# Block sums of V on TensorE, a first layer split 2, 3, 3, 4, and a floor under weights in an attention and two-layer MLP kernel

## The chip, the cores and the metric

The kernel runs on one core of one Trainium2 chip. The metric is device time in microseconds of one execution. Five engines work side by side, each on its own queue in order: TensorE (PE, with its weight loads as PEld), VectorE (DVE), ScalarE (ACT), GpSimd (POOL) and SyncE (SP), which here only starts transfers.

## The reference

The first stage is attention over 768 positions, for 2 batches of 8 heads of 64: each query sees the keys nearer than 16 positions, and 24 summaries, one per block of 32 positions (the maximum of the block's keys, the mean of its values). Two MLP layers follow on the 1536 tokens of width 512. The weights come as 64-bit floats.

```python
k_sum = k.reshape(B, H, nb, block, D).max(axis=3)
v_sum = v.reshape(B, H, nb, block, D).mean(axis=3)
...
scores_s = scores_s + np.log(block)
scores_l_m = np.where(mask_l, scores_l, -1000000000.0)
scores_all = np.concatenate([scores_l_m, scores_s], axis=-1)
...
a = a / (np.sum(a, axis=-1, keepdims=True) + 1e-09)
return np.matmul(a, v_all).astype(np.float32)
...
g = x @ w_gate
silu = g * (1.0 / (1.0 + np.exp(-g)))
val = x @ w_val
return (silu * val @ w_out).astype(np.float32)
...
h = x @ w_in
relu6 = np.clip(h + 3.0, 0.0, 6.0)
g = h * relu6 / 6.0
return (g @ w_out).astype(np.float32)
```

## The kernel before

**Attention.** Four tiles of 384 queries (two per batch), and in each four pairs of heads. A pair goes through: `scores` (24 matmuls on TensorE, tile `at_s`; `kT`, `ksum` and the queries, `acc` or `qT`), `top` (VectorE adds the mask and takes each row's extremum, six times), `exp` (ScalarE, six times), `norm` (VectorE), `weigh` (GpSimd multiplies P), `turn` (TensorE transposes P, `at_t`), `pt_put` (ScalarE copies it to `pt`), `outputs` (12 matmuls of P^T with the values `vw`, tile `pv`: a PV), and the output's split into `x` (ScalarE copies the high part, VectorE takes the rest). Per batch and pair there are also the maximum of the keys (`ksum`, VectorE) and the summaries of the values: VectorE sums V (`total`, tile `v`), TensorE turns the sums (`mm_v`, `at_v`), and ScalarE or VectorE copies them into `vw`.

**MLP.** Every product is made of three matmuls of high and low parts (`three`, L368 to L370), so that fp32 accuracy is kept. Layer one has 12 blocks of 128 hidden units, done in 4 groups of 3 blocks; the first group runs on the four tiles of 384 tokens as attention gives them, the other three on three tiles of 512. Layer two has 16 blocks in 4 groups of 4.

**Weights** (`weights`). A block of 128x512 64-bit values is loaded (`raw`, 3 buffers) and turned to fp32 bits (`bits`, 2 buffers) by steps on VectorE: the exponent (L405), the sign (L411), the tail (L415) and a guard (L423) that multiplies by 0 where the magnitude, which ScalarE takes in place (L419), is below 2^-15. Then the high part is copied and the low part taken (`wa` or `wb`, one ring per group in turn; `wb` exists only from the `swap` on, when attention's buffers are given up).

**The order.** Nothing runs in the order in which it is written. Every step is a task with a rank and a guess of its duration per engine; a planner (`Plan`) takes, engine by engine, the task that can start first, and of those the one of lowest rank, six rounds over. The instructions are issued in the order that comes out. Ranks come from the constants at the head (`LEAD`, `SPAN`, ...). Where the plan has TensorE idle in the first 60 us it puts dummy matmuls on zeros (L812).

Of the kernel before, what the change touches and what calls it, by code (L numbers as in the profile page):

```python
# [15 lines left out]
P = 128  # L16
# [17 lines left out]
F1, G1 = 1536 // P, 3  # L34
F2, G2 = 2048 // P, 4
N1, N2 = F1 // G1, F2 // G2
NEG = 1.0e9
SCALE = 1.0 / D**0.5


LEAD = dict(
    w_load=5.21, k_load=6.88, v_load=8.44, q_load=7.36, vw_load=1.00, keys=3.87, values=0.53, queries=2.61,
    k_put=1.0, v_put=1.0, q_put=1.0, top=3.0, exp=3.0, norm=4.0, weigh=4.0, turn=4.0, pt_put=4.0,
)
LAG = 2.58
MASKS = -5.01
PAIR_GAP = 4.06
MAIN = 28.05
W_FIRST = 6.44, 0.80
W_REST = 18.53, 3.46  # L50
SPAN = 12.44
NEXT, NEXT_END = -3.40, 23.95
NEXT_W = 7.71
W_END = 15.26
LATE = 0.90
# [3 lines left out]
BIAS = dict(dve=.4)  # L59
# [3 lines left out]
def consts():  # L63

    import numpy as np

    a = np.zeros((P, P + 3 * NK), np.float32)  # L70
# [29 lines left out]
class Task:  # L100
    __slots__ = ("engines", "port", "rank", "fn", "deps", "takes", "uses", "end", "engine", "start")


class Plan:
# [15 lines left out]
    def add(self, rank, engines, fn, r=(), w=(), after=(), port=False):  # L120
# [5 lines left out]
        t.port = {"pool": True, "dve": port}  # L126
        t.engines, t.rank, t.fn, t.end, t.takes = engines, rank, fn, None, []
# [46 lines left out]
    def schedule(self, rank):  # L174
# [14 lines left out]
        free, order, held = {}, [], {}  # L189
        while pool:  # L190
# [20 lines left out]
            s, t, e = best  # L211
            t.start, t.engine, t.end = s, e, s + t.engines[e]
# [68 lines left out]
def tile_kernel(ctx: ExitStack, tc: tile.TileContext, q, k, v, vu, w_gate, w_val, w_out1, w_in2, w_out2, cst, out):  # L281
    nc = tc.nc
    rings = dict(mm=4, mmb=4, at=3, pv=1, wa=9, wb=9, raw=3, bits=2, u=3, g=4, gb=5,
                 v3=1, qT=4, p=4, st=2, pt=4)
# [27 lines left out]
    for n in ("v3", "qT", "p", "st", "pt"):  # L312
        pools[n] = ab_p

    tiles = {}
    pv_bank = pools["pv"].tile([P, T], F32, name="pv")
# [17 lines left out]
    cs = cpool.tile([P, P + 3 * NK], F32, name="cs")  # L334
# [11 lines left out]
    def tiles_of(layer, g):  # L346
        nb = TB if (layer, g) == (0, 0) else WIDE
        return [(b0, nb) for b0 in range(0, BLOCKS, nb)]
# [9 lines left out]
    def three(rank, bk, n, lhs, rhs, n_k, reads, early=False):  # L358
# [35 lines left out]
    def weights(rank, layer, g, i, f, after):  # L394
# [4 lines left out]
        def load():  # L399
            src = w_src(layer, i, g * (G1, G2)[layer] + f)  # L400
# [57 lines left out]
    def hidden1(rank, g, t, f, late):  # L458
# [14 lines left out]
        for i, bk in enumerate((bg, bv)):  # L473
# [6 lines left out]
                early=g == 0 and b0 == 0,  # L480
# [7 lines left out]
    def out1(rank, g, t, d, late):  # L488
# [6 lines left out]
            G1,  # L495
# [4 lines left out]
        room = [("A", b0 // TB)] + [("q0", t, c) for t in range(2) for c in range(NP) if q_room(t, c) == b0 // TB] if g == 0 else []  # L500
# [49 lines left out]
    def out2(rank, g, t, m, late, d0=0, n=DM):  # L550
        if (g, m, n) == (N2 - 1, BLOCKS - 1, DM):
# [9 lines left out]
            G2,  # L561
# [22 lines left out]
    vw = [ap_.tile([NK, NB, P], F32, name=f"vw{c}") for c in range(NP)]  # L584
# [16 lines left out]
    def v_room(b, c):  # L601
        return c if b == 0 else 2 + c % 2

    def load_v(b, c):
        vn[b, c] = acc_room(v_room(b, c), 0, S)
        nc.sync.dma_start(out=vn[b, c], in_=v[b, c])

    def load_vw(t, c):
        b, half = divmod(t, 2)
        u0, to = half * NB, vw[c]  # L610
        nc.sync.dma_start(out=to[NS + HALO : NS + HALO + QB], in_=vu[b, c, :, u0 + 1 : u0 + 1 + NB])
        nc.sync.dma_start(out=to[NS : NS + HALO], in_=vu[b, c, QB - HALO :, u0 : u0 + NB])
        nc.sync.dma_start(out=to[NS + HALO + QB :], in_=vu[b, c, :HALO, u0 + 2 : u0 + 2 + NB])

    def keys(rank, b, c):
# [14 lines left out]
    def values(rank, b, c):  # L630
# [10 lines left out]

        def put(e):
            copy(e, vw[c][:NS], tiles[ps].unsqueeze(1).to_broadcast([NS, NB, P]), 1.0 / BLOCK)

        add(rank, {"dve": 0.87}, total, r=[room], w=[v3])
        add(rank, {"pe": 0.12}, turn, r=[v3, ("cs",)], w=[ps, ("vs", c)])
        add(rank - LEAD["v_put"], {"act": 0.69, "dve": 0.86}, put, r=[ps], w=[("vs", c)])

    def queries(rank, t, c):
        n = ("qT" if t > 1 else "q0", t, c)  # L650
        b, half = divmod(t, 2)

        def load():
            if t < 2:
                tiles[n] = acc_room(q_room(t, c), S + c % 2 * T, T)
            else:
                new(n, [P, T])
            second(t, c).dma_start(out=tiles[n], in_=q[b, c, :, half * T : (half + 1) * T])

        add(rank - LEAD["q_load"], {"dma": 0.68}, load, w=[n])  # L660

    def scores(rank, t, c):

        b, half, qt = t // 2, t % 2, ("qT" if t > 1 else "q0", t, c)
# [21 lines left out]
        for j in range(TR):  # L686
            add(rank, {"pe": 0.37}, lambda j=j: go(j), r=[("kT", b, c), ("ksum", c), qt],
# [230 lines left out]
```

## Time and profile before

| | |
|---|---|
| median of 3 runs | 632.81 us (632.78 to 635.15) |
| the profiled execution | 632.16 us, span of its instructions 630.4 us |
| TensorE busy | 618.9 us (98% of the span) |
| VectorE busy | 426.7 us (68%) |
| ScalarE busy | 269.2 us (43%) |
| GpSimd busy | 51.5 us (8%) |
| read from HBM, written | 50.19 MB, 3.15 MB |

Busy times are means over stages that differ; a duration of a matmul includes the part that lies under its neighbours, so what one costs is read from the distance of two starts. Dummy matmuls count as busy.

### The profile page before, as it was taken

What the parts mean: (1) busy time and instruction counts of PE and PEld (TensorE: products, weight loads), DVE (VectorE), ACT (ScalarE), POOL (GpSimd) and SP (SyncE); (2) the same over time, 40 slices, a digit from 0 to 9 for tenths busy, and PEclk for the clock granted to TensorE, in tenths of its full rate; (3) what the DMA queues carried; (4) which work ended last, traced back from release to release, by engine and by line L of the source; (5) the groups of instructions that cost most, each with busy time, mean ns of one, the idle gap of its engine ahead of it and who ended that gap; (6) DMA issues with size and microseconds to landing.
All of it is one profiled execution on the core that took longest, in us unless ns stands there. A gap on an engine that the chain in (4) does not pass through costs nothing.

```text
span 630.4 us, 10224 instructions
## 1 busy us (share of the span) xinstructions
PE 618.9 (98%) x3976; PEld 523.1 (83%) x3976; DVE 426.7 (68%) x881; ACT 269.2 (43%) x594; POOL 51.5 (8%) x55
## 2 busy tenths in 40 slices
PE   8899999999999999999999999999999999999997
PEld 7787889998888888888888888888888888888886
DVE  5999954799999847595739978565758553344332
ACT  4896886465545323242225444544523331132120
POOL 1333423001010000000000110000000000000000
PEclk9999999999999999999999999999999999999999
DMA  9887241233432403022011412030301000000103
GB/s 321 262 277 234 71 129 44 68 133 135 137 130 101 165 2 100 1 100 101 33 35 34 134 34 73 31 131 11 123 1 67 1 2 0 1 0 1 67 18 116
DMA packets 18912, 53.99 MB, mean 86 GB/s; under 512 B 2608, under 2 KB 5168, under 8 KB 18864
## 3 DMA queue, kind: packets, MB, share of 16 engines
q1 hardware_dynamic: 18576, 52.74, 24.7%
q8 instruction: 31, 0.51, 0.3%
q10 hardware_dynamic: 288, 0.61, 0.3%
q14 instruction: 17, 0.14, 0.1%
HBM read 50.19 MB, written 3.15 MB: 85 GB/s over the span
## 4 chain that ended last, share of the span: by engine, by line
PE 91%; DVE 5%; DMA 3%; issue 0%; ACT 0%
PE mm L368 16%; PE mm L369 15%; PE mm L370 15%; PE mmb L368 13%; PE mmb L369 13%; PE mmb L370 13%; PE at_s L681 2%; DMA kT<-in_k 1%; DMA raw<-in_moe_w_val 1%; PE pv L752 1%; PE at_t L738 1%; DVE p L701 1%; DVE bits L415 1%; DVE wa L302 0%; DVE ksum L623 0%
## 5 line engine op out<-in xcount | busy, mean ns | idle before, releaser
L368 PE MATMUL mm<-x,wa 128*128 128x384 f32 (+1 forms) x168 | 63.5, 378 | 0.0
L369 PE MATMUL mm<-x,wa 128*128 128x384 f32 (+1 forms) x168 | 61.0, 363 | 1.4 <-DVE wa L302 1.4
L370 PE MATMUL mm<-x,wa 128*128 128x384 f32 (+1 forms) x168 | 60.9, 362 | 0.0
L419 ACT ACTIVATE raw<-raw 128x512 f32<-128x512 f32 x68 | 46.0, 678 | 33.2 <-DVE bits L411 33.0
L415 DVE SCALAR_TENSOR_TENSOR bits<-raw,bits 128x512 uint32<-128x512 uint32 x68 | 48.8, 722 | 0.1
L423 DVE SCALAR_TENSOR_TENSOR bits<-raw,bits 128x512 f32<-128x512 f32 x68 | 47.6, 704 | 0.8
L411 DVE SCALAR_TENSOR_TENSOR bits<-raw,bits 128x512 uint32<-128x512 uint32 x68 | 46.5, 685 | 0.7
L369 PE MATMUL mmb<-x,wb 128*128 128x512 f32 x120 | 46.7, 389 | 0.0
L370 PE MATMUL mmb<-x,wb 128*128 128x512 f32 x120 | 46.7, 389 | 0.0
L368 PE MATMUL mmb<-x,wb 128*128 128x512 f32 x120 | 46.7, 389 | 0.0
L368 PE MATMUL mm<-x,wb 128*128 128x512 f32 x120 | 46.7, 389 | 0.0
L369 PE MATMUL mm<-x,wb 128*128 128x512 f32 x120 | 46.7, 389 | 0.0
L370 PE MATMUL mm<-x,wb 128*128 128x512 f32 x120 | 46.7, 389 | 0.0
L708 ACT ACTIVATE p<-p,st 128x120 f32<-128x120 f32 x96 | 36.6, 383 | 5.1 <-DVE st L701 5.1
L368 PE MATMUL mmb<-x,wa 128*128 128x512 f32 (+1 forms) x96 | 36.7, 382 | 0.0
L369 PE MATMUL mmb<-x,wa 128*128 128x512 f32 (+1 forms) x96 | 36.7, 382 | 0.0
L370 PE MATMUL mmb<-x,wa 128*128 128x512 f32 (+1 forms) x96 | 36.7, 382 | 0.0
L369 PEld LDWEIGHTS mm<-x,wa 128*128 128x128 f32 x168 | 31.6, 188 | 5.2 <-DVE wa L302 1.9
L295 ACT ACTIVATE wb<-bits 128x512 fp32r<-128x512 f32 x32 | 20.2, 632 | 36.4 <-PE mm L370 14.9
L571 DVE SCALAR_TENSOR_TENSOR acc<-mmb,acc 128x512 f32<-128x512 f32 (+1 forms) x19 | 12.9, 676 | 33.7 <-PE mmb L370 33.6
L295 ACT ACTIVATE wa<-bits 128x512 fp32r<-128x512 f32 x33 | 20.8, 631 | 34.4 <-DVE bits L423 13.7
L368 PEld LDWEIGHTS mm<-x,wa 128*128 128x128 f32 x168 | 31.5, 188 | 4.7
(1462 smaller groups left out, 1496.1 us busy)
## 6 DMA issues: line engine op xcount, KB each, us to landing
raw<-in_moe_w_out SPq DMA_DIRECT2D x28, 512.0 KB, 3.3
raw<-in_moe_w_in SPq DMA_DIRECT2D x16, 512.0 KB, 3.2
raw<-in_moe_w_gate SPq DMA_DIRECT2D x12, 512.0 KB, 3.4
raw<-in_moe_w_val SPq DMA_DIRECT2D x12, 512.0 KB, 3.4
acc<-in_v SPq DMA_DIRECT2D x8, 384.0 KB, 5.2
vw<-in_vu SPq DMA_DIRECT2D x16, 192.0 KB, 4.2
out<-acc SPq DMA_DIRECT2D x11, 256.0 KB, 2.0
kT<-in_k SPq DMA_DIRECT2D x7, 400.0 KB, 5.5
```

Source lines behind the costliest of these rows:

```text
L295: nc.scalar.activation(dst, src, AF.Copy, scale=scale)
L368: nc.tensor.matmul(ps, lhsT=lh, rhs=rh, start=j == 0, stop=False)
L369: nc.tensor.matmul(ps, lhsT=ll, rhs=rh, start=False, stop=False)
L370: nc.tensor.matmul(ps, lhsT=lh, rhs=rl, start=False, stop=j == n_k - 1)
L411: nc.vector.scalar_tensor_tensor(t, high_w(), 0xC0000000, t, ALU.bitwise_and, ALU.bitwise_or)
L415: nc.vector.scalar_tensor_tensor(t, low_w(), 29, t, ALU.logical_shift_right, ALU.bitwise_or)
L419: nc.scalar.activation(mag, mag, AF.Abs)
L423: nc.vector.scalar_tensor_tensor(as_f(), mag, 2.0**-15, as_f(), ALU.is_ge, ALU.mult)
L571: nc.vector.scalar_tensor_tensor(a, tiles[bk][:, :n], 1.0 / 6.0, a, ALU.mult, ALU.add)
L681: nc.tensor.matmul(tiles["at", "s", *names[h]][a * QB : (a + 1) * QB, j, cols], lhsT=tiles[qt][hs, u * QB : (u + 1) * QB], rhs=rhs, start= ...
L701: nc.vector.tensor_tensor_reduce(out=tiles[p][:, r, :], in0=tiles[ps][:, r, :], in1=cs[:, P + kind * NK : P + (kind + 1) * NK], scale=-SCA ...
L708: nc.scalar.activation(a, a, AF.Exp, bias=s[:, 0, n : n + 1], scale=-1.0, accum_out=s[:, 1, n : n + 1])
```

## The change

The summaries of V in the first batch are made by TensorE: V is loaded with positions on partitions (`vr`), and six matmuls with a constant matrix of 1/32 sum it (`means`). The second batch keeps the reduction on VectorE. Layer one's 12 blocks are done in groups of 2, 3, 3 and 4. The weights go to `wa` and `wb` by nines, whatever their group. The magnitude now goes to `bits` first, is raised to at least 2^-15 (`floor`) and then shifted; the fourth VectorE step on two tensors is gone. The planner adds 0.12 and 0.1 us where TensorE goes to or leaves scores, every rank constant is new, and tasks and rooms are written for tiles of any size (here they stay four of 384). Of the table of ranks the diff shows a line or two.

```diff
+ATT = (0, 0, 6), (0, 6, 6), (1, 0, 6), (1, 6, 6)
+V_PE = True, False
-F1, G1 = 1536 // P, 3
-F2, G2 = 2048 // P, 4
+SIZES = (2, 3, 3, 4), (4, 4, 4, 4)
+SLOTS = 9
-MASKS = -5.01
+MASKS = -180.51
-MAIN = 28.05
+M_RANK = 125.37, 176.29, 194.29, 234.58
+SWITCH = {"S": 0.12}
+LEAVE = {"S": 0.1}
...
+    for n in range(P // BLOCK):
+        a[n * BLOCK : (n + 1) * BLOCK, P + NS - P // BLOCK + n] = 1.0 / BLOCK
...
+    elif name == "vr":
+        a = a.reshape(B, NP, 2, CHUNKS, P, D).transpose(0, 1, 4, 3, 2, 5).reshape(B, NP, P, S)
...
             s, t, e = best
+            if e == "pe" and t.kind != kind:
+                s += SWITCH.get(t.kind, 0.0) + LEAVE.get(kind, 0.0)
+                kind = t.kind
...
+    for layer in range(2):
+        for g in range(len(SIZES[layer])):
+            for i, f in order_of(layer, g):
+                w_names[layer, g, i, f] = ("wa" if len(w_names) // SLOTS % 2 == 0 else "wb", layer, g, i, f)
...
+        def size():
+            nc.scalar.activation(new(bits, [P, 512], U32).bitcast(F32), high_w().bitcast(F32), AF.Abs)
+
+        def floor():
+            nc.vector.tensor_scalar(as_f(), as_f(), 2.0**-15, None, ALU.max)
+
         def exponent():
-            nc.vector.tensor_scalar(
-                new(bits, [P, 512], U32), high_w(), 3, 0x3FFFFFF8, ALU.logical_shift_left, ALU.bitwise_and
-            )
+            t = tiles[bits]
+            nc.vector.tensor_scalar(t, t, 3, 0x3FFFFFF8, ALU.logical_shift_left, ALU.bitwise_and)
...
-        def size():
-            mag = high_w().bitcast(F32)
-            nc.scalar.activation(mag, mag, AF.Abs)
-
-        def guard():
-            mag = high_w().bitcast(F32)
-            nc.vector.scalar_tensor_tensor(as_f(), mag, 2.0**-15, as_f(), ALU.is_ge, ALU.mult)
...
+        def means():
+            tiles[ps] = new_bank(ps, [NS, P])
+            for i in range(CHUNKS):
+                c0 = P + NS - (i + 1) * (P // BLOCK)
+                nc.tensor.matmul(tiles[ps], lhsT=cs[:, c0 : c0 + NS], rhs=vn[b, c][:, i * P : (i + 1) * P],
+                                 start=i == 0, stop=i == CHUNKS - 1)
...
+        if V_PE[b]:
+            add(rank, {"pe": 1.35}, means, r=[room, ("cs",)], w=[ps, ("vs", c)], kind="V")
+        else:
+            add(rank, {"dve": 0.87}, total, r=[room], w=[v3])
+            add(rank, {"pe": 0.12}, turn, r=[v3, ("cs",)], w=[ps, ("vs", c)], kind="T")
...
         def load():
-            second(2 * b, c).dma_start(out=kT[b, c], in_=k[b, c])
+            second(2 * b, c).dma_start(out=new(n, [P, S + 2 * HALO]), in_=k[b, c])
```

The order shows three places. First TensorE, from the scores of the first pair (`at_s_0`) to the first pair's transposes (`at_t_0`), with the turned or summed V (`mm_v`) and dummies (`mm_none`); before:

```order
L681 MATMUL at_s_0_1_165<-kT_0_100,acc 64x96
...
L640 MATMUL mm_v_0_201<-cs,v_0_0_193 24x128
...
L681 MATMUL at_s_1_0_237<-ksum_97,acc 64x24
...
L640 MATMUL mm_v_1_278<-cs,v_0_1_261 24x128
...
L738 MATMUL at_t_0_0_314<-cs,p_0_0_164 120x128 x3
...
L738 MATMUL at_t_0_1_324<-cs,p_0_1_166 120x128 x3
```

and in the change:

```order
L720 MATMUL at_s_1_1_224<-kT_1_150,acc 64x96
...
L677 MATMUL mm_v_0_269<-acc,cs 24x128 x6
L777 MATMUL at_t_0_0_290<-cs,p_0_0_168 120x128 x3
...
L777 MATMUL at_t_0_1_299<-cs,p_0_1_170 120x128 x3
L720 MATMUL at_s_2_0_309<-ksum_98,acc 64x24
```

The sum of V's first pair now is six matmuls that stand behind the second pair's scores and just ahead of the first transposes; of the dummies behind the first batch of 42 (50 in the change) 110 stood in the program, and 37 do.

Second VectorE, from the third pair's first row maximum (`p_2_0`) on, where the first weight blocks (`bits_0_0_0`, `bits_0_1_0`) begin; before:

```order
L636 TENSOR_REDUCE v_0_2_353<-acc 128x24
L405 TENSOR_SCALAR bits_0_0_0_388<-raw_0_0_0_286 128x512
L302 TENSOR_TENSOR x<-pv,x 128x3x128
L701 ISA p_2_0_331,st_2_329<-at_s_2_0_330,cs 128x120
...
L411 SCALAR_TENSOR_TENSOR bits_0_0_0_388<-raw_0_0_0_286,bits_0_0_0_388 128x512
L623 TENSOR_REDUCE ksum_99<-kT_3_103 128x24
```

and in the change:

```order
L740 ISA p_2_0_310,st_2_308<-at_s_2_0_309,cs 128x120
...
L436 TENSOR_SCALAR bits_0_1_0_344<-bits_0_1_0_344 128x512
L440 TENSOR_SCALAR bits_0_1_0_344<-bits_0_1_0_344 128x512
L444 SCALAR_TENSOR_TENSOR bits_0_1_0_344<-raw_0_1_0_256,bits_0_1_0_344 128x512
L448 SCALAR_TENSOR_TENSOR bits_0_1_0_344<-raw_0_1_0_256,bits_0_1_0_344 128x512
L759 TENSOR_SCALAR st_2_308<-st_2_308 128x6
```

The reduction of V (L636) is gone from here, the third pair's maxima stand ahead of the first weight block, and a block is two short steps and two long ones, side by side.

Third SyncE, the head of the queue (`cs` the constants, `kT` keys, `acc` queries and values); before:

```order
L795 DMA cs<-in_cst 128x360
```

stood fifth, behind the first constants, keys, queries and values, and in the change the queue begins:

```order
L835 DMA cs<-in_cst 128x360
L832 DMA cs<-in_cst 128x172
L651 DMA kT_0_147<-in_k 128x800
L697 DMA acc<-in_q 128x384
L651 DMA kT_2_154<-in_k 128x800
```

The masks (128x360) went ahead of everything, and the first constants grew from 128 to 172 columns.

## Rows read from the trace of the kernel before

**Rows 1.** Windows: length, PE, PEld, DVE, ACT, POOL busy us, granted clock, DMA, GB/s

```profile
7.00:27.00 20.00, 17.19 (x374) 14.68 (x370) 17.98 (x72) 15.52 (x60) 5.49 (x6) 1.00 0.92 304
20.00:40.00 20.00, 17.36 (x357) 14.47 (x357) 19.28 (x72) 17.73 (x62) 5.31 (x6) 1.00 0.80 249
27.00:54.30 27.30, 25.13 (x419) 21.11 (x418) 26.60 (x93) 22.81 (x78) 9.60 (x11) 1.00 0.84 273
54.30:73.00 18.70, 17.71 (x229) 15.68 (x230) 18.63 (x52) 13.97 (x42) 8.46 (x8) 1.00 0.45 135
73.00:109.00 36.00, 36.00 (x581) 31.69 (x575) 20.36 (x104) 27.44 (x104) 11.14 (x14) 1.00 0.28 90
109.00:626.50 517.50, 517.50 (x2342) 434.97 (x2343) 341.33 (x561) 188.16 (x312) 16.41 (x12) 1.00 0.18 62
```

**Rows 2.** Timeline of TensorE: start us, duration us, engine, line, operation

```profile
6.65 0.42 PE L681 MATMUL at_s<-ksum,acc 64*64 64x24 f32 x8 [0.99 <-DVE ksum L623]
...
28.92 0.38 PE L681 MATMUL at_s<-kT,acc 64*64 64x96 f32 x8
29.11 0.26 PE L681 MATMUL at_s<-ksum,acc 64*64 64x24 f32 x8
...
41.37 0.49 PE L738 MATMUL at_t<-cs,p 128*120 128x128 f32 x3
41.61 0.42 PE L368 MATMUL mm<-x,wa 128*128 128x384 f32 x1
41.87 0.34 PE L369 MATMUL mm<-x,wa 128*128 128x384 f32 x1
42.04 0.34 PE L370 MATMUL mm<-x,wa 128*128 128x384 f32 x1
...
53.44 0.92 PE L752 MATMUL pv<-pt,vw 120*64 120x64 f32 x24
54.29 0.44 PE L368 MATMUL mm<-x,wa 128*128 128x384 f32 x1
...
223.95 0.39 PE L368 MATMUL mm<-x,wa 128*128 128x512 f32 x1
...
225.31 0.39 PE L368 MATMUL mm<-x,wa 128*128 128x512 f32 x1
```

**Rows 3.** Line of the dummies, 8 to 60 us: durations in ns, first and last start

```profile
L812 PEld LDWEIGHTS <-zeros x110: 95/98/152, 8.5 to 48.3; 128*128 128x128 bf16 x110
```

**Rows 4.** Timelines of VectorE, and of GpSimd beside it

```profile
5.64 0.95 DVE L623 TENSOR_REDUCE ksum<-kT 128x24 f32<-128x768 f32 x1 [5.64 <-DMA kT<-in_k]
...
22.17 1.28 DVE L415 SCALAR_TENSOR_TENSOR bits<-raw,bits 128x512 uint32<-128x512 uint32 x1
...
31.03 0.42 DVE L405 TENSOR_SCALAR bits<-raw 128x512 uint32<-128x512 uint32 x1
31.37 0.28 DVE L701 CUSTOM_DVE_ANT_0 p<-at_s,cs 128x120 f32<-128x120 f32 x1
...
31.57 0.69 DVE L411 SCALAR_TENSOR_TENSOR bits<-raw,bits 128x512 uint32<-128x512 uint32 x1
32.18 0.42 DVE L405 TENSOR_SCALAR bits<-raw 128x512 uint32<-128x512 uint32 x1
...
49.21 0.19 DVE L721 RECIPROCAL st<-st 128x6 f32<-128x6 f32 x1
...
21.85 2.24 POOL L732 TENSOR_TENSOR p<-p,st 128x360 f32<-128x360 f32 x2 [4.35 <-ACT raw L419]
```

**Rows 5.** Timeline of ScalarE

```profile
9.53 0.80 ACT L295 ACTIVATE vw<-mm_v 24x768 f32<-24x768 f32 x1 [6.60 <-PE mm_v L640]
10.24 0.38 ACT L708 ACTIVATE p<-p,st 128x120 f32<-128x120 f32 x1
...
52.06 0.87 ACT L295 ACTIVATE pt<-at_t 120x384 f32<-120x384 f32 x2
```

**Rows 6.** Timeline of TensorE, its wait for a weight block

```profile
50.02 0.44 PE L369 MATMUL mm<-x,wa 128*128 128x384 f32 x1 [1.03 <-DVE wa L302]
```

**Rows 7.** Timeline of SyncE, its first two issues

```profile
0.73 0.38 SPq L792 DMA_DIRECT2D cs<-in_cst  x1
1.17 0.42 SPq L620 DMA_DIRECT2D kT<-in_k  x1
```

More of the change, by code (lines that the diff above doesn't have):

```diff
@@ L58 @@
 FILL = 60.0
-BIAS = dict(dve=.4)
+BIAS = dict(dve=0.54)
 ROUNDS = 6
@@ L100 @@
 class Task:
-    __slots__ = ("engines", "port", "rank", "fn", "deps", "takes", "uses", "end", "engine", "start")
+    __slots__ = ("kind", "engines", "port", "rank", "fn", "deps", "takes", "uses", "end", "engine", "start")
 class Plan:
@@ L118, in __init__, with add @@
         self.tasks, self.last, self.readers, self.users = [], {}, {}, {}
-    def add(self, rank, engines, fn, r=(), w=(), after=(), port=False):
+    def add(self, rank, engines, fn, r=(), w=(), after=(), port=False, kind=None):
         t = Task()
         t.port = {"pool": True, "dve": port}
+        t.kind = kind
         t.engines, t.rank, t.fn, t.end, t.takes = engines, rank, fn, None, []
@@ L188, in schedule @@
         pool = [t for t in self.tasks if not left[t]]
-        free, order, held = {}, [], {}
+        free, order, held, kind = {}, [], {}, None
         while pool:
@@ L311, in tile_kernel @@
     pools["pv"] = pool("pv", att, space=PSUM)
-    for n in ("v3", "qT", "p", "st", "pt"):
+    for n in ("v3", "kT", "qT", "p", "st", "pt"):
         pools[n] = ab_p
     tiles = {}
-    pv_bank = pools["pv"].tile([P, T], F32, name="pv")
+    pv_bank = pools["pv"].tile([P, MU * QB], F32, name="pv")
     def new(name, shape, dtype=F32):
@@ L346, in tiles_of @@
     def tiles_of(layer, g):
-        nb = TB if (layer, g) == (0, 0) else WIDE
-        return [(b0, nb) for b0 in range(0, BLOCKS, nb)]
+        if (layer, g) == (0, 0):
+            return [(b * CHUNKS + u0 // 2, n // 2) for b, u0, n in ATT]
+        return [(b0, WIDE) for b0 in range(0, BLOCKS, WIDE)]
     banks = [0]
@@ L718, in go @@
         def go():
-            s = tiles[st]
-            nc.vector.tensor_scalar(s[:, 2, :], s[:, 1, :], 1.0e-9, None, ALU.add)
-            nc.vector.reciprocal(s[:, 3, :], s[:, 2, :])
-        add(rank - LEAD["norm"], {"dve": 0.37}, go, r=[("exp", t, c, h, r) for h in range(2) for r in range(TR)], w=[st], port=True)
+            s, n = tiles[st], ATT[t][2]
+            nc.vector.tensor_scalar(s[:, 2, :n], s[:, 1, :n], 1.0e-9, None, ALU.add)
+            nc.vector.reciprocal(s[:, 3, :n], s[:, 2, :n])
@@ L725, in head @@
+        add(rank - LEAD["norm"], {"dve": 0.37}, go, r=[("exp", t, c, h, r) for h in range(2) for r in range(ATT[t][2] // 2)], w=[st], port=True)
     def head(rank, t, c, h):
-        x = (t, c, h)
+        x, rows = (t, c, h), ATT[t][2] // 2
         p, st, tp, pt = ("p", *x), ("st", t, c), ("at", "t", *x), ("pt", *x)
         def weigh(e):
-            f = tiles[st][:, 3, h * TR : (h + 1) * TR].unsqueeze(2).to_broadcast([P, TR, NK])
+            f = tiles[st][:, 3, h * rows : (h + 1) * rows].unsqueeze(2).to_broadcast([P, rows, NK])
@@ L732, in weigh @@
             eng[e].tensor_tensor(tiles[p], tiles[p], f, ALU.mult)
         def turn():
-            s = tiles[tp] = new_bank(tp, [P, TR, P])[:NK]
-            new(pt, [NK, TR, P])
-            for r in range(TR):
+            s = tiles[tp] = new_bank(tp, [P, rows, P])[:NK]
+            tiles[pt] = new(pt, [NK, MU // 2, P])[:, :rows]
+            for r in range(rows):
                 nc.tensor.transpose(s[:, r, :], tiles[p][:, r, :], ident)
-        add(rank - LEAD["weigh"], {"pool": 0.76, "dve": 0.45}, weigh, r=[st], w=[p], port=True)
@@ L744, in outputs @@
     def outputs(rank, t, c):
         pv, pts = ("pv", t, c), [("pt", t, c, h) for h in range(2)]
+        b0, nb = tiles_of(0, 0)[t]
         def weighted():
-            tiles[pv] = pv_bank
-            for u in range(NB):
+            tiles[pv] = pv_bank[:, : nb * P]
+            for u in range(2 * nb):
                 for h in range(2):
@@ L844, in next_weights, with span_of, change @@
     def next_weights(layer, g, rank, span):
-        order = order1 if layer == 0 else order2
+        order = order_of(layer, g)
         for n, (i, f) in enumerate(order):
-            weights(rank + span * n / len(order), layer, g, i, f, (swap,))
-    def span_of(layer, t):
-        n = t[1] * P / 2400 + 0.0135
-        return (2 * G1 * KC * 3 * n, KC * G1 * 3 * n) if layer == 0 else (G2 * KC * 3 * n, t[1] * G2 * 0.69)
+            weights(rank + span * n / len(order), layer, g, i, f, (swap,) if w_name(layer, g, i, f)[0] == "wb" else ())
+    def span_of(layer, g, t):
+        n = 3 * (t[1] * P / 2400 + 0.0135)
+        return (2 * SIZES[0][g] * KC * n, KC * SIZES[0][g] * n) if layer == 0 else (SIZES[1][g] * KC * n, t[1] * SIZES[1][g] * 0.68)
+    def change():
+        att.close()
+        pools["wb"] = pool("wb")
+        pools["gb"] = pool("gb")
+        pools["mmb"] = pool("mmb", space=PSUM)
     seq = [(layer, g, t) for layer, groups in ((0, N1), (1, N2)) for g in range(groups) for t in tiles_of(layer, g)]
-    for layer, g, t in seq + [(2, 0, None)]:
+    for step_no, (layer, g, t) in enumerate(seq + [(2, 0, None)]):
         late, span = swap is not None, sum(p[0] for p in prev)
+        if step_no < NT:
+            rank = M_RANK[step_no]
         if layer == 0:
-            heads_ = [lambda r, f=f: hidden1(r, g, t, f, late) for f in range(G1)]
+            heads_ = [lambda r, f=f: hidden1(r, g, t, f, late) for f in range(SIZES[0][g])]
         elif layer == 1:
-            heads_ = [lambda r, f=f: hidden2(r, g, t, f, late) for f in range(G2)]
+            heads_ = [lambda r, f=f: hidden2(r, g, t, f, late) for f in range(SIZES[1][g])]
         else:
```

219 lines of the change are left out of this document (111 added, 108 removed).

## Prediction

> **What bounds the kernel now.** I read the windows first. From 73 us to 626.5 us TensorE is busy all the time (36.00 of 36.00 us, 517.50 of 517.50) [rows 1]: whatever the other engines do there costs nothing, and a matmul that starts every 0.173 us (384 columns) or 0.227 us (512 columns; 1.36 us for six) sets the time [rows 2]. The last 3.9 us are the tail. So the end is where it is because of the work that TensorE has left when it first runs without holes, and because of when that is. The holes lie ahead of 73 us. I mark the point with the eighth PV matmul group (second tile of queries, fourth pair of heads), which starts at 53.44 us [rows 2].
>
> Is the count closed? By the order of its instructions TensorE has, after PV 8, 375 matmuls of 384 columns (65.1 us), 2112 of 512 (478.8), 24 of 256 at half the 0.227 (2.7), 8 score groups at 0.85 (6.8), 48 transposes at 0.083 (4.0), 8 PV at 0.85 (6.8), 4 turned sums at 0.2 (0.8), and 66 changes from one kind to another at 0.09 (5.9; a matmul behind a transpose takes 0.26 us to the next, in a run 0.17) [rows 2]. That is 570.9 us; from PV 8's end (54.29) to the last matmuls (626.5) it took 572.2. So only 1.3 us behind PV 8 are stalls.
>
> Ahead of PV 8 the same prices give 31 us of useful work in 53.4 us. The rest is the wait for the first scores (6.65 us) and holes, which the kernel fills with 110 dummy matmuls (8.5 to 48.3 us) [rows 3]. What makes the holes? VectorE: 17.98 of 20 us, 26.60 of 27.3 us busy [rows 1]. Up to the last norm that PV 8 needs (49.21) I count 39.0 us of work on it (8 reductions at 0.87, 48 row maxima at 0.20, 22 weight steps of two tensors, 4 of them residuals, at 0.6, 7 short weight steps at 0.34, and 6.7 of norms, outputs and others) in the 43.8 us since its first instruction at 5.64: 0.89 [rows 4]. ScalarE comes next: up to the last P^T copy for PV 8 it has 48 exponentials at 0.376, 16 copies of P^T and 7 of the output at 0.375, 3 of the sums at 0.7, 6 sizes at 0.57, 5 weight copies at 0.53 and 3 others at 0.375, 35.9 us in the 43.4 us from 9.53 to 52.93: 0.83 [rows 5]. And close ahead of PV 8 the chain is one of weights: TensorE waits 1.0 us for a weight residual of VectorE, at 50.02 [rows 6].
>
> **The change, part by part.** *Sums of V on TensorE* (first batch). Four reductions (0.87 us each) leave VectorE, 3.5 us; four turned sums (0.2 us) leave TensorE, and 24 matmuls of 128 columns in fp32 come. No row shows one. Below: a transpose of 128 columns, 0.083, so 0.5 us for six. Above: PV, two 64-column halves in 0.142, so 0.284 for 128 columns, 1.7 us for six. The nearest is four scores of 96 columns side by side in 0.19 us [rows 2], scaled by columns 0.25: 1.5 us per pair, and 5.2 us more in all. They stand where dummies stood; the cover is the holes, and gone it costs these 5.2 us (a rival below).
>
> *Groups of 2, 3, 3, 4.* Ahead of the end of attention six weight blocks are needed, not nine, and of the first layer's work ahead of PV 8 only 36 matmuls stand there, not 57. The two-tensor weight steps that VectorE does ahead of PV 8's last norm fall from 22 to 7 (the fourth step is gone, residuals are with GpSimd, and fewer blocks are due). At its rows' prices VectorE's 39.0 us become 28.5: 6 reductions, 48 maxima, 8 norms at 0.32, 7 long and 9 short weight steps, 6 outputs at 0.47, 1 copy of 0.87.
>
> *The guard as a maximum.* Per block VectorE loses one step of 0.6 us and gains one of 0.34 [rows 4]: 0.26 us, 18 us over 68 blocks, of which only the first few lie where VectorE sets anything; behind 73 us TensorE covers it all. ScalarE's size is the same instruction with another output, but now it comes first: a block waits for it once more.
>
> GpSimd takes over residuals: four ahead of PV 8, where it had none. While it worked on P (21.85 to 24.09), a two-tensor step of VectorE took 1.28 us, not 0.69 [rows 4]; four residuals could hold up VectorE by 0.6 us each, 2.4 us on 28.5, which stays below ScalarE. [...]
>
> *Queue.* The masks (184 KB) and a longer first constant now stand ahead of the first K on SyncE's queue, one issue (0.44 us) later [rows 7], and 0.2 MB at 304 GB/s [rows 1] is 0.7 us, in part beside it: +0.7 us on the first reduction (6.3), so the first scores end at 8.3 and the first exponential starts near 8.6, where 10.24 stood: it waits for no reduced V in front of it on VectorE, and for no copy of the sums on ScalarE.
>
> *What is late next* is ScalarE. Its work ahead of PV 8 barely shrinks: 50 exponentials, 16 and 7 copies, 3 sums, 5 sizes, 3 weight copies, 1 other, 34.35 us. How dense can it run? Not above 1 (42.9 us for PV 8); it ran at 0.83 behind a full VectorE (50.0); its densest window has 17.73 of 20 us, 0.89 [rows 1], and the engine that bound this stage reached 0.89. I take 0.87, a little below: 39.5 us, and PV 8 at 48.1 us, 5.3 us earlier.
>
> *Behind PV 8* the same count of TensorE for the change: 252 matmuls of 384 (43.7), 2220 of 512 (503.3), 2.7, 6 score groups (5.1), 4.0, 6.8, 0.8, 56 changes of kind (5.0): 571.4 us, 0.5 us more. Stalls: 1.3 us before. There now ScalarE has 38 us beside 43.5 us of TensorE up to the last PV (0.87), where it had 27.44 of 36 [rows 1], and each pair's chain is covered by two blocks of matmuls, not three. None would be 1.3 us back; the window from 54.3 to 73 us shows 1 us in 18.7 with VectorE full, and twice that rate is 4 us. I take 1.0 more.
>
> *Weights of the second group*, costed at nothing: three blocks are made ahead of the swap of pools, six behind it. From the last PV TensorE still has 126 matmuls of 384 (21.9 us) and three blocks of 12 (8.2): the fourth block is wanted 30 us later. If that cover went, a stall of a block's making, some 3 us, would come.
>
> **Sum.** -5.3 + 0.5 + 1.0 = -3.8 us on the profiled execution's 632.16 us (span 630.4 and 1.8 around it), 628.4; the median shown, 632.81, lies 0.65 higher, so **629.0 us**.
>
> **Rivals.** *Given back behind PV 8*: the start shortens, but tiles three and four starve TensorE by 4 to 6 us instead of 1. For it: ScalarE at 0.87. Against it: at 0.75 there was no stall at all [rows 1]. 632 to 634 us, no change.
> *The sums of V lie on the path* (the other side): between the scores and the transposes of each pair TensorE keeps its holes and the 24 matmuls come on top. Then PV 8 starts at 7.35 + 32.6 (useful work ahead of it) + 15.7 (before's holes since 6.65) = 55.7, 2.2 us later, and with 0.5 and a stall of 1 the time is 636.5. It decides if PV 8 comes later than 53.4. For it: they stand ahead of the transposes in TensorE's order; against it: 110 dummies stood in the holes of this stretch [rows 3].
> [...]
>
> **Chances.** Forecast (PV 8 some 3 to 8 us earlier, few stalls) 0.62, with its own range 625 to 631.5; given back 0.20; sums of V on the path 0.12; clock 0.06. Half a per cent, 3.2 us, is about what a measurement tells from no change: under 629.6 us lie 0.85 of the forecast and a little of the rest, 0.54; above 636 us most of the third and half of the last and some of the second, 0.16; 0.30 between. Range: 0.95 of ScalarE's time gives PV 8 at 44.8 and 625; upward it takes in the second rival, to 634.5.
>
> **What would show it.** Right: PV 8 near 48 us, ScalarE's share there near 0.87 and VectorE's well below 0.97; six sums of V in some 1.5 us; first scores near 7.3 us; TensorE full from about 60 us on, and from the last PV (about 93 us) without a wait for weights. Wrong: PV 8 later than 52 us; idle time of TensorE behind PV 8 above 4 us, ended by ScalarE or GpSimd; a wait for a weight block between 100 and 200 us; a granted clock under 1.

## The result, and the profile after

The changed kernel takes 625.51 us (median of four runs, 625.08 to 625.72), the kernel before beside it 632.79 us: a ratio of 0.9881 with a 95% interval of 0.985 to 0.9912. 629.0 was forecast, with a range of 625.0 to 634.5. The profiled execution takes 625.37 us with a span of 623.6, against 632.16 and 630.4.

The windows, in the stretches of [rows 1] (length, busy us of PE, PEld, DVE, ACT and POOL, granted clock, DMA share, GB/s):

```profile
7.00:27.00 20.00, 18.50 (x383) 15.25 (x384) 15.25 (x75) 16.38 (x63) 6.99 (x9) 0.91 0.97 308
20.00:40.00 20.00, 19.72 (x427) 16.87 (x424) 16.10 (x75) 18.82 (x68) 10.36 (x11) 1.00 0.86 251
27.00:54.30 27.30, 27.25 (x492) 24.14 (x491) 24.03 (x109) 25.87 (x98) 12.53 (x14) 1.00 0.82 254
54.30:73.00 18.70, 18.65 (x356) 16.14 (x355) 16.44 (x64) 17.29 (x60) 9.22 (x10) 1.00 0.74 233
73.00:109.00 36.00, 36.00 (x371) 33.98 (x372) 29.05 (x87) 27.41 (x79) 7.75 (x9) 1.00 0.25 83
109.00:619.00 510.00, 510.00 (x2265) 423.31 (x2264) 319.01 (x545) 178.62 (x295) 9.55 (x7) 1.00 0.18 61
```

TensorE, which had 2.17 us free between 27 and 54.3 us and 0.99 between 54.3 and 73, has none that counts behind 27 us. VectorE fell from 0.97 to 0.88 of the third stretch, ScalarE rose from 0.84 to 0.95. The waits of TensorE in the whole run (us in total, times, longest) are four, where [rows 2, 6] showed two of those of before:

```profile
PE at_s L720 <- DVE ksum L654: 2.1, 1, 2.1
PE mm_none L852 <- POOL zeros L845: 1.0, 1, 1.0
PE at_t L777 <- DVE st L740: 0.3, 1, 0.3
PE at_t L777 <- POOL p L771: 0.2, 1, 0.2
```

The two large ones lie ahead of 8 us. The marks of the prediction, from TensorE's timeline (start, duration, operation); the first reduction and the first exponential are from those of VectorE and ScalarE:

```profile
6.79 1.81 DVE L654 TENSOR_REDUCE ksum<-kT 128x24 f32<-128x768 f32 x2 [6.79 <-DMA kT<-in_k]
9.78 0.40 ACT L747 ACTIVATE p<-p,st 128x120 f32<-128x120 f32 x1 [6.85 <-DVE st L740]
```

```profile
7.80 0.31 PE L720 MATMUL at_s<-ksum,acc 64*64 64x24 f32 x8 [2.08 <-DVE ksum L654]
...
12.83 1.49 PE L677 MATMUL mm_v<-acc,cs 128*24 128x128 f32 x12
...
48.39 0.92 PE L792 MATMUL pv<-pt,vw 120*64 120x64 f32 x24
...
91.07 0.92 PE L792 MATMUL pv<-pt,vw 120*64 120x64 f32 x24
...
620.04 0.28 PE L387 MATMUL mmb<-wb,g_(8, 4)_3_5569 128*128 128x256 f32 x1
```

PV 8 starts at 48.39 us, 5.05 earlier than in [rows 2]. From there to the start of the last matmul it is 571.65 us (before: 573.16, from 53.44 to 626.60), and 3.56 to the end of the span (before 3.80). So:

| | before | after | difference | forecast |
|---|---|---|---|---|
| start of PV 8 | 53.44 | 48.39 | -5.05 | -5.3 |
| PV 8 to the last matmul's start | 573.16 | 571.65 | -1.51 | +0.5 (work) +1.0 (stalls) |
| from there to the end of the span | 3.80 | 3.56 | -0.24 | 0 |
| span | 630.4 | 623.6 | -6.8 | -3.8 |

### The profile page after: what moved, and what is told of

It is laid out like the page before. It is cut to its first block, busy times and chain, and to the rows that moved or that the text cites. A ratio compares the mean times of both kernels' runs of the same rounds, so it can differ in the third digit from the quotient of the medians.

```text
span 623.6 us, 10039 instructions
## 1 busy us (share of the span) xinstructions
PE 616.4 (99%) x3919; PEld 518.4 (83%) x3919; DVE 405.4 (65%) x877; ACT 266.8 (43%) x591; POOL 46.4 (7%) x53
## 4 chain that ended last, share of the span: by engine, by line
PE 97%; DVE 1%; DMA 1%; POOL 0%; issue 0%; SPq 0%; POOLq 0%; DVEq 0%
PE mm L385 16%; PE mm L386 16%; PE mm L387 16%; PE mmb L386 14%; PE mmb L387 14%; PE mmb L385 14%; PE at_s L720 3%; PE pv L792 2%; PE at_t L777 2%; DMA kT<-in_k 1%; DVE p L740 1%; POOL p L771 0%; PE mm_none L852 0%; PE at_v L677 0%; PE mm_v L677 0%
## 5 line engine op out<-in xcount | busy, mean ns | idle before, releaser
L385 PE MATMUL mm<-x,wa 128*128 128x512 f32 (+1 forms) x152 | 58.3, 384 | 0.0
L387 PE MATMUL mm<-x,wa 128*128 128x512 f32 (+1 forms) x152 | 56.2, 369 | 0.0
L386 PE MATMUL mm<-x,wa 128*128 128x512 f32 (+1 forms) x152 | 56.1, 369 | 0.0
L433 ACT ACTIVATE bits<-raw 128x512 f32<-128x512 f32 x68 | 45.4, 674 | 22.2 <-DVE wa L318 10.0
L386 PE MATMUL mmb<-x,wa 128*128 128x512 f32 (+1 forms) x140 | 54.1, 386 | 0.0
L387 PE MATMUL mmb<-x,wa 128*128 128x512 f32 (+1 forms) x140 | 54.0, 386 | 0.0
L385 PE MATMUL mmb<-x,wa 128*128 128x512 f32 (+1 forms) x140 | 54.0, 386 | 0.0
L318 POOL TENSOR_TENSOR wb<-bits,wb 128x512 fp32r<-128x512 f32 x6 | 8.1, 1345 | 349.8 <-ACT wb L311 232.9
L385 PE MATMUL mmb<-x,wb 128*128 128x512 f32 x84 | 32.7, 389 | 0.0
L386 PE MATMUL mmb<-x,wb 128*128 128x512 f32 x84 | 32.7, 389 | 0.0
L387 PE MATMUL mmb<-x,wb 128*128 128x512 f32 x84 | 32.7, 389 | 0.0
L385 PEld LDWEIGHTS mm<-x,wa 128*128 128x128 f32 x152 | 28.5, 188 | 4.7
L386 PEld LDWEIGHTS mm<-x,wa 128*128 128x128 f32 x152 | 28.6, 188 | 3.8
L387 PEld LDWEIGHTS mm<-x,wa 128*128 128x128 f32 x152 | 28.5, 188 | 3.7
L436 DVE TENSOR_SCALAR bits<-bits 128x512 f32<-128x512 f32 x68 | 29.3, 432 | 2.4 <-ACT bits L433 2.2
```

The source lines that it names most:

```text
L385: nc.tensor.matmul(ps, lhsT=lh, rhs=rh, start=j == 0, stop=False)
L386: nc.tensor.matmul(ps, lhsT=ll, rhs=rh, start=False, stop=False)
L387: nc.tensor.matmul(ps, lhsT=lh, rhs=rl, start=False, stop=j == n_k - 1)
L433: nc.scalar.activation(new(bits, [P, 512], U32).bitcast(F32), high_w().bitcast(F32), AF.Abs)
L436: nc.vector.tensor_scalar(as_f(), as_f(), 2.0**-15, None, ALU.max)
```

## The experiments

All start from the changed kernel. In the table the times are in us, the ratio is to the kernel before, timed beside each; first PV, PV 8 and the last matmul are starts in the profiled execution, and the last three columns are what TensorE loses there in three stretches: its idle time, with the distance that dummies take up, added up from its timeline. A wait counts whole in the stretch in which it ends, so the column 7-23 has the whole wait for the first scores (2.08 us in the changed kernel, 2.59 in after_again).

| kernel | median (runs) | ratio, 95% interval | first PV | PV 8 | last matmul | 7-23 | 23-49 | 49-74 |
|---|---|---|---|---|---|---|---|---|
| before | 632.79 | 1 | 16.02 | 53.44 | 626.60 | 7.7 | 4.4 | 2.0 |
| after | 625.51 (4) | 0.9881, 0.985-0.9912 | 19.70 | 48.39 | 620.04 | 6.2 | 0.3 | 0 |
| after_again | 626.38 (6) | 0.9922, 0.9895-0.995 | 18.42 | 48.52 | 620.16 | 6.2 | 1.4 | 0 |
| v_vector | 630.15 (5) | 0.9959, 0.9947-0.9971 | 18.53 | 51.36 | 624.79 | 8.9 | 3.7 | 2.4 |
| groups_3333 | 633.45 (12) | 1.0021, 1.0006-1.0036 | 18.29 | 48.93 | 626.92 | 5.1 | 1.8 | 4.5 |
| guard_mult | 631.80 (11) | 0.9993, 0.9985-1.0002 | 19.57 | 55.42 | 626.46 | 6.3 | 2.2 | 2.1 |
| v_both | 631.71 (11) | 0.9997, 0.9984-1.0011 | 18.11 | 48.54 | 625.17 | 4.7 | 0.3 | 0 |
| plan_blind | 628.36 (6) | 0.995, 0.9931-0.9968 | 19.80 | 50.66 | 622.22 | 6.5 | 1.0 | 0 |
| all_undone | 633.84 (9) | 1.003, 1.002-1.004 | 19.31 | 51.67 | 628.12 | 9.7 | 3.7 | 3.5 |
| floor_twice | 629.07 (6) | 0.9943, 0.9928-0.9958 | 19.44 | 50.28 | 623.47 | 6.8 | 1.8 | 0.9 |
| v_sum_also | 627.33 (6) | 0.9924, 0.9908-0.9941 | 21.55 | 51.40 | 623.06 | 7.0 | 1.5 | 0.3 |
| no_floor | 625.64 (4) | 0.9899, 0.9882-0.9915 | 18.30 | 48.94 | 620.59 | 5.1 | 2.0 | 0 |
| warm_start | 624.23 (6) | 0.9888, 0.9867-0.9908 | 18.24 | 47.12 | 618.79 | 3.8 | 0.3 | 0 |
| few_dummies | 627.68 (6) | 0.9926, 0.9909-0.9943 | 19.07 | 48.71 | 620.38 | 3.6 | 0.6 | 0 |

The changed kernel stands there twice. The two measurements lie 0.9 us apart by the medians and 0.0041 (2.6 us) by the ratios, so no difference to it below is known better than that.

### Each part undone, the plan free to choose another order

**v_vector**, the sums of V back on VectorE:

```diff
-V_PE = True, False
+V_PE = False, False
```

> The changed kernel with the sums of V of the first batch back on VectorE (four reductions of 0.87 us and four turned sums). Theory (ScalarE sets the start, and VectorE has slack there): VectorE has 32.4 us of work ahead of PV 8 where the changed kernel has 28.5, ScalarE still 34 to 35; PV 8 comes within 1.5 us of the changed kernel's 48.4 us, and the time is 625.5 to 627. Rival (the start is still VectorE's): its 3.9 us appear in full, PV 8 at 52, time 629 to 629.5. Second rival (the sums lie on TensorE's path at the start): PV 8 up to 2 us earlier, 623.5 to 625.

4.6 us more than the changed kernel, PV 8 2.97 later. My theory missed. The numbers are near those of the first rival (PV 8 at 52, 629 to 629.5), but the plan also put other work ahead of PV 8 (39 matmuls of 384 columns, not 36), so they don't prove it. TensorE has 5.3 us less work (24 matmuls at 1.42 us per six, less four turned sums) and loses 8.5 us more between 7 and 74 us. The second rival of the experiment, that the sums stood in TensorE's way, is out.

**groups_3333**:

```diff
-SIZES = (2, 3, 3, 4), (4, 4, 4, 4)
+SIZES = (3, 3, 3, 3), (4, 4, 4, 4)
```

> The changed kernel with the first layer's groups 3, 3, 3, 3. By the order of instructions every engine does the same up to PV 8, so PV 8 stays at 48.4 us under every theory. Theory (the group of 2 is what keeps TensorE fed behind PV 8, since six weight blocks and not nine are due there): TensorE's counted work behind PV 8 falls by 0.5 us, but holes come, 26 dummies' worth by the plan (2.4 us) and more where weights are late; time 627 to 630. Rival (the group size is worth nothing behind PV 8, and the stalls went by the new order of the attention alone): no holes, 625.0.

PV 8 is where it was, 0.5 us off, and 4.5 us of holes stand behind it where the changed kernel has none. Waits of TensorE between 49 and 74 us, those that are on VectorE or on weights:

```profile
PE at_v L671 <- DVE st L740: 1.3, 1, 1.3
PE mm L386 <- DVE wa L318: 0.5, 1, 0.5
...
PE mm L385 <- ACT wa L311: 0.2, 1, 0.2
```

The holes came, as the theory had it, and its price was low: 7.9 us by the medians, 6.9 by the last matmul, not 2 to 5. That they come of nine weight blocks due instead of six is shown only for the 0.7 us of waits on `wa`. The longest wait, 1.3 us, is put down to VectorE's row maxima, and some 2 us of the loss lie in no hole.

**guard_mult**, the old guard (`floor` gone, `exponent` from the raw block, and at the end):

```diff
+        def guard():
+            mag = high_w().bitcast(F32)
+            nc.vector.scalar_tensor_tensor(as_f(), mag, 2.0**-15, as_f(), ALU.is_ge, ALU.mult)
...
+        add(rank, {"act": 0.58}, size, w=[raw])
```

> The changed kernel with the old guard (a comparison and product over two tensors on VectorE at the end of each weight block, ScalarE's size in place in the raw block). Theory (0.26 us per block, few blocks ahead of PV 8, ScalarE sets the start): two to three us of VectorE's work come ahead of PV 8, hidden for the most part; PV 8 at 48.5 to 50, time 625.5 to 627.5. Rival (the guard is a main part, since it is where VectorE is again near 0.95 full): PV 8 at 52 or later, time 629 or more.

The rival's numbers: 6.3 us more, PV 8 at 55.42. But the plan put other work ahead of PV 8 as well (48 matmuls of 384, not 36), so this run alone doesn't say whether load or order did it.

**v_both**, the second batch's sums on TensorE too:

```diff
-V_PE = True, False
+V_PE = True, True
```

> The changed kernel with the sums of V of the second batch on TensorE too: 24 matmuls in place of four turned sums, behind PV 8, where TensorE has no holes. Theory (what TensorE gets behind PV 8 is paid in full): 4 times 1.42 us less 4 times 0.07 to 0.2 us, so 4.9 to 5.4 us more, time 630.4 to 631; PV 8 stays at 48.4. Rival (VectorE is still the bound behind PV 8, and 3.5 us of its relief shorten the chains): less than 2 us more, 625.5 to 627.5.

6.2 us more by the medians, 5.1 by the last matmul, PV 8 in place. One of the sums stands right ahead of it (TensorE's timeline):

```profile
47.12 1.49 PE L677 MATMUL at_v<-acc,cs 128*24 128x128 f32 x12
48.54 0.92 PE L792 MATMUL pv<-pt,vw 120*64 120x64 f32 x24
```

Where TensorE has no holes, the same matmuls that pay in the first batch cost their whole price (5.1 us, where 4.9 to 5.4 was reckoned).

### The order, and all parts at once

**plan_blind**: only the plan's prices for changes of kind are gone.

```diff
-SWITCH = {"S": 0.12}
-LEAVE = {"S": 0.1}
+SWITCH = {}
+LEAVE = {}
```

> The changed kernel with the plan's prices for changes of kind on TensorE set to nothing: the same instructions in another order. Theory (parts carry the gain): at most 1.5 us more, 625 to 627. Rival (the gain needs an order that is fitted to its inputs, and any change of what the plan reckons with loses it): 4 to 8 us more, 629.5 to 633.5, with holes of TensorE between 7 and 73 us.

2.9 us more by the medians, 2.2 by the last matmul: between the two. The intervals of this kernel and of after_again meet, so its worth lies between nothing and some 3 us.

**all_undone**: the edits of v_vector, groups_3333, guard_mult and plan_blind together.

> The changed kernel with sums of V on VectorE, groups of 3, the old guard and no prices for changes of kind: the work of the kernel before under the new ranks and lead times. If the losses of the parts undone singly were each the worth of a part, they add: 4.6 + 7.9 + 6.3 = 18.8 us, 644. Theory (each of those losses is mostly that of an order which no longer fits): far less than the sum, 630 to 637.

8.3 us more than the changed kernel, where the single losses of the first three add to 18.8 (plan_blind's is not counted). So what one part's removal costs under ranks that were chosen for all parts is not that part's worth. This kernel is also 0.3% slower than before: the new ranks and the new order of loads alone gain nothing.

### VectorE's load with the order held fixed

Here every engine's other instructions stay in the changed kernel's order.

**floor_twice** and **no_floor**:

```diff
         def floor():
-            nc.vector.tensor_scalar(as_f(), as_f(), 2.0**-15, None, ALU.max)
+            for _ in range(2):                     # floor_twice; no_floor: pass
+                nc.vector.tensor_scalar(as_f(), as_f(), 2.0**-15, None, ALU.max)
```

> The changed kernel with each weight block's maximum done twice on VectorE, and every other instruction in the same order on every engine: 0.34 us more per block, 1.7 us ahead of PV 8, which is more than the 0.26 us that the old guard cost. Theory (the undone guard lost 6.3 us through the order that the plan then chose, not through its load): under 1 us more, 625 to 626.5, PV 8 at 48.4 to 49.5. Rival (VectorE's load as such sets the start): its 1.7 us and stalls behind it, 627.5 to 632.

> The changed kernel without the maximum of each weight block (the guard for very small weights is left out), everything else in the same order: 0.34 us less of VectorE per block, 1.7 us less ahead of PV 8. Theory (behind the first 20 us the changed kernel is bound by TensorE, and more load on VectorE costs because it opens holes, while less gains nothing): 625 to 626, PV 8 within 0.5 us. Rival (VectorE still sets the start, so that less load gains as much as more cost): PV 8 1.5 to 2 us earlier, 622 to 624.

no_floor went as the theory had it: 625.64 us, no gain. Its first seven PV groups start within 0.15 us of those of warm_start (below), which has the full load; then TensorE stops for 1.69 us ahead of PV 8 (TensorE's timeline of no_floor):

```profile
48.33 0.40 PE L720 MATMUL at_s<-kT,qT 64*64 64x96 f32 x8 [1.69 <-issue]
```

floor_twice is 3.6 us longer (2.7 against after_again), the rival's figure, and the theory of under 1 us missed. Its trace says from where: up to the sixth PV it is 0.1 us behind the changed kernel (40.42 against 40.33), or 0.35 counted from the first PV, which is 0.26 earlier. Then come 1.53 us in which TensorE waits for nothing that the profile shows (the last section is on such stops), and 0.9 us of waits for VectorE and ScalarE near 60 us. Timeline of TensorE, and its waits between 50 and 74 us:

```profile
40.42 0.85 PE L793 MATMUL pv<-pt,vw 120*64 120x64 f32 x21
42.81 0.33 PE L793 MATMUL pv<-pt,vw 120*64 120x64 f32 x3 [1.53 <-issue]
...
PE at_t L778 <- DVE st L741: 0.6, 1, 0.6
PE at_v L672 <- ACT pt L311: 0.3, 1, 0.3
```

So 1.7 us more on VectorE cost 0.1 to 0.35 us before that stop. Whether VectorE's load has a part in the stop is open.

**v_sum_also**:

```diff
         def means():
+            total()
             tiles[ps] = new_bank(ps, [NS, P])
```

> The changed kernel with the four reductions of V done on VectorE as well, their result unused, at the places where TensorE does the sums, every other instruction in the same order: 3.5 us more on VectorE ahead of PV 4, TensorE's load as in the changed kernel. Theory (VectorE has some 3 us of 21 free between 27 and 48 us; ScalarE sets the pace): 0.5 to 2 us more, 626 to 627.5. Rival (VectorE's load sets it): 3.5 us or more, 629 or later. If it gives as much as the kernel with the sums back on VectorE alone (630.15), that loss was VectorE's load; if much less, it was the order.

1.0 us above after_again by the medians, within both intervals; in its trace PV 3 to the last matmul are 3.0 us later than in the changed kernel. The first PV is already 1.85 later, and the granted clock between 7 and 27 us is 0.83, not 0.91. How much of the 3.0 is the reductions' and how much the clock's is open. By the measure set beforehand, 627.33 is well short of v_vector's 630.15 and speaks for the order as the greater part of that loss; the traces don't settle it, since PV 8 starts at 51.40 here and at 51.36 in v_vector.

### The start: clock and dummies

**after_again** is the changed kernel unchanged, **warm_start** has 16 more dummies ahead of the first scores, **few_dummies** lacks the 37 behind them:

```diff
-    def idle(n=IDLE, bk=none):
+    def idle(n=IDLE + 16, bk=none):               # warm_start
...
-FILL = 60.0
+FILL = 5.0                                        # few_dummies
```

> The changed kernel once more, beside the three below on one chip: 625 to 626 under every theory. Its first scores wait about 2 us for the first reduction and the granted clock falls behind that wait, or, if the wait is nearer 1.5 us, it stays at 1.00.

> The changed kernel with 16 more dummy matmuls ahead of the first scores, everything else in the same order: they end at 6.7 to 7.5 us, so that the wait for the first reduction falls from 2.1 us to under 1.2. Theory (the fallen clock costs: in two kernels with the same order and a wait of 1.5 us or less the first PV starts 1.4 to 1.6 us earlier): granted clock 1.00 between 7 and 27 us, first PV near 18.2 us, 1 to 1.6 us less, 624 to 624.6. Rival (the dip lies in time that TensorE waits anyway; of the changed kernel's runs those at a mean clock of 1.00 are not shorter): the same time within 0.4 us, 625 to 626.

> The changed kernel without the 37 dummy matmuls behind the first scores, everything else in the same order. Theory (they keep the granted clock up while TensorE has holes): the clock between 7 and 27 us falls below the 0.91 of the changed kernel, first PV 1 to 3 us later, 626.5 to 628.5. Rival (they stand in the way: 15 of them take 1.7 us ahead of the second pair's scores): first PV up to 1.5 us earlier, 624 to 625.5.

The profiled execution of the changed kernel shows a fall of the granted clock to 0.50 (windows of 1 us, columns as above):

```profile
8.00:9.00 1.00, 1.00 (x44) 1.00 (x41) 0.60 (x1) 0.00 (x0) 0.00 (x0) 0.57 1.05 396
9.00:10.00 1.00, 1.00 (x18) 0.78 (x14) 0.55 (x5) 0.22 (x1) 0.00 (x0) 0.50 1.03 393
10.00:11.00 1.00, 1.00 (x11) 0.87 (x9) 1.00 (x9) 1.00 (x7) 0.00 (x0) 0.50 1.05 413
11.00:12.00 1.00, 1.00 (x46) 0.93 (x44) 0.62 (x1) 1.00 (x7) 0.00 (x0) 0.72 0.98 383
```

It follows the 2.08 us wait for the first reduction, and the clock rose again while TensorE was busy (1.00 us of each of these four). In after_again the clock stayed at 1.00 although that wait was 2.59 us, so my tie between the wait's length and the fall missed. Its first PV is 1.28 us earlier; the four rows lack 1.7 us of full clock, so I put about that 1.3 down to the fall, as an estimate. But these two profiled executions take the same time (625.37 and 625.51 us), since TensorE stops later for 1.14 us, in the middle of a PV group, with no wait that the profile shows. Timeline of after_again, then of warm_start at the same place:

```profile
39.05 0.85 PE L792 MATMUL pv<-pt,vw 120*64 120x64 f32 x21
41.04 0.33 PE L792 MATMUL pv<-pt,vw 120*64 120x64 f32 x3 [1.14 <-issue]
41.30 0.44 PE L385 MATMUL mm<-x,wa 128*128 128x384 f32 x1
```

```profile
39.05 0.92 PE L792 MATMUL pv<-pt,vw 120*64 120x64 f32 x24
39.89 0.44 PE L385 MATMUL mm<-x,wa 128*128 128x384 f32 x1
```

warm_start had neither the fall nor the stop: PV 8 at 47.12, 624.23 us. That is the fastest of all, lowest run 623.90 against 625.08; but two of its six runs lie at 626.6 and 627.4, and its interval overlaps that of after_again, so the gain of about 1.3 us is seen in the trace and not settled by the times. few_dummies is undecided in its time: its granted clock is 0.91 in the profile, as in the changed kernel, its first PV 0.63 us earlier, and its ratio that of after_again.

The mean granted clock of every run, which stands beside its time, says more than the two profiles. The kernel before ran 55 times beside the experiments: 20 runs with a mean of 0.996 or 0.997 have a median of 632.74 us, 35 with 0.999 or 1.00 one of 631.63. So a run with the lower mean is there about 1.1 us longer. The first four runs of the changed kernel don't show it (625.37 and 625.08 us at 0.996 and 0.997, 625.66 and 625.72 at 1.00); the six of after_again do (625.1 to 625.8 at 1.00, 627.0 and 627.6 at 0.997, 630.9 at 0.992). None of few_dummies' six runs has 1.00 (0.993 to 0.997), where five of the changed kernel's ten and five of warm_start's six have it: with more dummies the mean clock was under 1.00 less often, as the theory of few_dummies had it.

## Why the prediction came out, and which step was off

**The start of PV 8 (forecast -5.3, measured -5.05) holds in size, not in its limiter.** I let ScalarE set it, 34.35 us of work from 8.6 us on at a share of 0.87. The first exponential came at 9.78, 1.2 us late (the first scores at 7.80, not 7.3, and then at a granted clock of 0.50 to 0.72), and ScalarE ran denser: up to the end of the last P^T copy for PV 8, 0.90 by the same count of work. Timeline of ScalarE:

```profile
47.61 0.48 ACT L311 ACTIVATE pt<-at_t 120x384 f32<-120x384 f32 x1
```

The two errors cancel. And the wait that ends last is not ScalarE's: between 23 and 49 us TensorE lost 0.3 us. In the chain of waits of the changed kernel from 22.6 us to PV 8 nearly every piece is TensorE's own (the share of its lines between 22 and 49 us):

```profile
by line: PE at_s L720 23.4%; PE pv L792 17.8%; PE at_t L777 15.2%; PE mm L385 10.0%; PE mm L387 7.8%; PE mm L386 7.7%; DVE p L740 7.1%; PE mm_v L677 5.3%; PE at_v L677 5.3%; issue 0.9%; DVE st L740 0.4%; DVEq L740 0.0%
```

I expected TensorE to be full from 60 us; it is full from 23. no_floor shows it from the other side: relief of VectorE gains nothing any more (625.64 us against 625.51).

**The mis-sized term is "Stalls +1.0 behind PV 8".** The count of TensorE's work there was 571.4 us; it took 570.9 (571.65 less PV 8's own 0.85, and 0.12 for the last matmul), where before 572.4 stood against 570.9. So the stalls went from +1.5 to -0.5, by 2.0 us, and the half below nothing is error of the count's prices. The windows show 0.9 of the 2.0 us as idle time (TensorE's free time between 54.3 and 73 us fell from 0.99 to 0.05); the rest lies in the distances of matmuls and may be error of the prices as well. My reason for more stalls was that two blocks of matmuls cover a pair's chain worse than three. groups_3333 shows the opposite, in an order planned anew behind PV 8: with three blocks due TensorE loses 4.5 us between 49 and 74 us, with two nothing. The tail's -0.24 was not reckoned, and is not explained. The work term of +0.5 cannot be told apart from the stalls. The lower end of the range was also off by its own terms: PV 8 at 44.8 gives 625.7 us, not 625, once the 0.65 of the sum is added, and the measured 625.51 lies just under that.

**The sums of V** cost 1.42 us per pair between starts (1.5 forecast). That they lie in holes is shown by v_vector and v_both: without them on TensorE the kernel is 4.6 us slower, though dummies take their place, and the same kind of work added where there are no holes makes the last matmul 5.1 us later.

**The guard** I held to be hidden but for the first few blocks. At a fixed order the trace of floor_twice bears that out up to the sixth PV (0.1 to 0.35 us for 1.7), and the rest of its loss is in two later places; the 6.3 us of guard_mult come with another order and are no measure of it.

**GpSimd's residuals** did not lengthen the stage: behind 8 us TensorE waited 0.2 us for GpSimd. The 0.6 us each by which they could hold up VectorE did not come: up to PV 8 none of its weight steps runs beside a residual, and one is longer beside GpSimd's work on P, 0.63 us where the others of its line up to there take 0.42 (timeline of VectorE):

```profile
32.60 0.63 DVE L436 TENSOR_SCALAR bits<-bits 128x512 f32<-128x512 f32 x1
```

**The rivals.** Given back behind PV 8: did not occur. Sums of V on the path: out. The clock (0.06 of the chances): the fall came, to 0.50 (in one of two profiles; five of ten runs have a mean clock under 1.00), and cost an estimated 1.3 us at the first PV; a loss of several us by it is shown in no profile. Weights of the second group: no wait for them, as forecast.

What stays open is how the start's 5 us divide among the parts. The runs show that undoing the sums, the groups or the guard alone doesn't leave the gain whole (ratios 0.9959 to 1.0021), with the plan free to choose another order, and that the losses don't add; with a planner that reorders everything, there may be no such division.

## What to carry to other kernels

Look at the holes of the engine whose work is fixed, stretch by stretch: extra work in a stretch with dummies can pay (without it the kernel was 4.6 us slower, in an order planned anew) and the same work 25 us later costs its whole price (5.1 us by the last matmul). When an order is planned, test a part at a fixed order too (double the suspect, then drop it), because undoing it under ranks tuned for the whole measures the ranks: 18.8 us in single losses were 8.3 together. And when a number comes out right, check the limiter: mine was right by two errors.

## What the hardware showed that I had not expected

TensorE stops with nothing to wait for that the profile shows. In eight places of seven traces (1.14 us in after_again, 1.53 in floor_twice, 1.69 in no_floor, 0.28 and 1.23 in groups_3333, 0.45 in few_dummies, 0.36 in v_vector, 0.98 before) it stops so between two instructions. The page counts 31 transfers on an instruction queue:

```profile
q8 instruction: 31, 0.51, 0.3%
```

That is 16.4 KB each. Each transfer's start is known to 0.13 us from the windows of the DMA queues. Every one of the eight stops ends 2.4 to 2.8 us after such a start: in after_again 38.25 and 41.04, in floor_twice 40.12 and 42.81, in no_floor 45.62 and 48.33, before 18.5 and 20.99. In warm_start, which didn't stop, the transfer ahead of that place started at 35.12, 4.8 us before it. The DMA engines are 0.92 to 0.96 busy in the stretches (7 to 27 us before, 27 to 48 in the others) in which the stops begin; v_vector's begins at 49.29, and between 48 and 50 us they are 1.00 busy there. They are as busy in warm_start (0.96), so that alone doesn't make a stop.

The counts of instructions suggest whose they are. The traces have 7869 instructions of TensorE in few_dummies with 30 transfers, 7941 to 8058 in twelve others with 31, and 8139 in all_undone with 32: one transfer for 254 to 262. And the seven stops of the changed kernel and its variants end after 1218 (few_dummies), 1473 (after_again, floor_twice, the first of groups_3333) or 1730 of them (no_floor, v_vector, the second of groups_3333): steps of 255 and 257, though few_dummies and v_vector have other instructions at these places. The one of before, after 616, is not on this grid.

That TensorE waits for its own instructions, which arrive late among the loads, is my guess: it fits these numbers, and no run shows it. It would also explain why an earlier start is sometimes lost again. Of the 1 to 2 us by which runs of one kernel differ the clock has a part (1.1 us in before); what the stops add is not shown.
